# Another order of the steps in a fused attention and token-mixing kernel: loads, stores, filling products and the engines of small copies

## The chip, the cores and the metric

The kernel runs on one core of a Trainium2 chip. The core has five engines that run side by side, each with its own queue of instructions: TensorE (matrix products, PE in the profile, its weight loads PEld), VectorE (DVE), ScalarE (ACT), GpSimd (POOL) and SyncE (SP), which here only issues transfers. An engine works its queue in order: an instruction that waits holds up everything behind it on that engine. Sixteen DMA engines move data between HBM and the on-chip memory; transfers are issued from the queues of SyncE, ScalarE and GpSimd. TensorE's results land in eight banks of PSUM and have to be copied out by VectorE or ScalarE. The metric is the time of one execution in microseconds (us), the median of several runs.

## The reference

Eight batches, eight heads, 576 tokens, 64 channels a head; 32 packed queries p a head. Cut to what matters:

```
def sm_attn(qq, kk, vv):
    s = scale * np.matmul(qq, kk.transpose(0, 1, 3, 2))
    a = np.exp(s - np.max(s, axis=-1, keepdims=True))
    a = a / (np.sum(a, axis=-1, keepdims=True) + 1e-09)
    return np.matmul(a, vv)
p_packed = sm_attn(p, k, v)            # 32 packed rows a head
out = sm_attn(q, p_packed, p_packed)   # 576 rows a head
x = out.transpose(0, 2, 1, 3).reshape(B, S, H * D)
wq, wk = x @ w_q, x @ w_k              # 512 -> 64
W_tok = scale * einsum('bsd,btd->bst', wq, wk)
mixed = einsum('bst,btd->bsd', W_tok, x)
result = np.maximum(mixed, 0.0) @ w_out
```

All inputs and the result are float32: q, k and v are 9.4 MB each, the result is 9.4 MB.

## The kernel before, in words

The kernel never forms W_tok; per batch it multiplies small matrices in another association. Its whole program is one written list, `ORDER`: each word is a step, `NAME.batch.part@engine=banks`, issued in that order, so the list sets the order on every engine's queue, while semaphores keep the data dependences between engines. No scheduler changes it. Engines are A (ScalarE), V (VectorE), P (GpSimd); a load without a mark is GpSimd's, a store without one SyncE's. A step on TensorE names the PSUM banks that it writes.

The steps of one batch b, in the order of its data:

- LD.k, LD.v, LD.q (line 154): loads, float32 in HBM, bf16 on chip, all issued from GpSimd's queue. There are four buffers of each. In batch 0 (h, g, r, q) and batch 7 (r, q) a load is cut in halves. LD.O loads the output weights.
- KT (line 255, VectorE): transposes K in blocks. S1 (263, TensorE): scores of the packed queries. X1 (287, ScalarE): exponentials, in two parts into a single buffer. TE (295, VectorE): transposes them. PV (306): product with V and row sums. RC and PP (318, 321, VectorE): division, and the mask of heads. PT (326): transpose.
- QK (331, TensorE): packed rows times both weight matrices; QKE (341) copies the result out of PSUM, QD (344, GpSimd) doubles a part of it.
- QV (351, VectorE): transposes Q. S2 (362, TensorE): scores of Q, in parts of two token groups (.0, .1), one (.2) or four (.3). X2 (375, ScalarE): exponentials. RS and RR (390, 396, VectorE): row sums and reciprocals. In batch 5 HA (385, GpSimd) first adds halves of the rows. AM (401, GpSimd, in one case VectorE): normalises. AT (409, TensorE): transposes the result. AE (421): copies it out.
- WKQ (433): the products with w_k and w_q; WE (456) copies them out. GM (461) and GE (470): the small matrix of the mixer and its copy. Y (473) and YE (481): the next one. MX (488) and MR (494): mixed rows, MR those of the last, remaining rows of a token group; RL, RLF (515, 519) and RLR (522): relu while copying out.
- OT (527): product with the output weights, 128 rows a step, two steps sharing two banks; part 4 is the remainder rows of two batches at once. OE, OEF (545, 548): copies out. ST, STF (555, 590): stores. In batch 7 the last 128 rows are cut in two column pieces, OH, OEH and STH (574, 581, 585), by the table `OHC` in line 11.

`WARM.n=bank` (line 611) is filling: products of a zero tile with itself, n units of 128 columns, whose result nobody reads. `WARM.n.128` issues them 128 columns at a time, otherwise 512.

`HOLD.v7` (line 567) issues a tiny transfer on SyncE's queue that reads the last V buffer, so every store behind it in that queue waits until V of batch 7 has landed. Copies named with line 128 or 132 in the profile are those of the helper `copy` (ScalarE and VectorE), transposes with line 237 those of `blocks`.

Of the kernel before, what the change touches and what calls it, by code (L numbers as in the profile page):

```python
# [650 lines left out]
```

## Time and profile before

| what | us |
|---|---|
| median of 3 runs (104.35 to 104.62) | 104.36 |
| the profiled execution | 104.42 |
| its span, first to last instruction | 102.6 |
| TensorE busy | 93.2 |
| of it filling products (line 617) | 20.0 |
| VectorE busy | 73.5 |
| ScalarE busy | 65.0 |
| GpSimd busy | 53.1 |

The page divides the span in 40 slices of 2.6 us and shows, for each, the busy share of every engine in tenths, the granted clock of TensorE, the busy share of the DMA engines and the GB/s. In lists of groups, a row has the line and engine, the names of output and inputs, how many instructions, their busy time and mean duration, and the idle time in front of them with what ended it. In a timeline a row begins with start and duration; the bracket at its end is the idle time of the engine before it and who ended that. In a table of windows the columns are the length, the busy time of PE, PEld, DVE, ACT and POOL with their instructions, the granted clock, the DMA share and GB/s.

### The profile page before, as it was taken

The page shows a single profiled execution, that of the slowest core. Times are in us where ns is not written, and L with a number is a line of the kernel's source. Part 1 is how long each engine was busy: PE and PEld are TensorE (multiplying, and loading weights), DVE is VectorE, ACT ScalarE, POOL GpSimd, SP SyncE. Part 2 cuts the span into 40 slices and gives each one's busy share as a digit, 9 for nine tenths or more (in the row PEclk, how much of TensorE's full clock was granted, in tenths as well). Part 3 has the DMA queues.
Part 4 walks back from the last instruction along what each step waited for, and adds up shares of the span by engine and source line. Part 5 has one row for each costly group of instructions (what it writes and reads, how often), then busy time and mean ns, then how long its engine had stood idle before and what let it go on. Part 6 is the DMA issues. An engine that isn't in the chain of part 4 may idle for free.

```text
span 102.6 us, 3594 instructions
## 1 busy us (share of the span) xinstructions
PE 93.2 (91%) x1536; PEld 55.1 (54%) x1536; DVE 73.5 (72%) x140; ACT 65.0 (63%) x111; POOL 53.1 (52%) x83
## 2 busy tenths in 40 slices
PE   5998999998699999999998899989999999999930
...
DMA  1999999999999999999999999999999999997893
GB/s 18 234 230 207 211 215 209 207 210 213 203 212 207 214 209 209 213 210 207 212 210 208 211 212 204 216 211 205 250 250 387 412 413 409 417 388 294 346 370 127
DMA packets 13567, 25.13 MB, mean 245 GB/s; under 512 B 1072, under 2 KB 6448, under 8 KB 13552
## 3 DMA queue, kind: packets, MB, share of 16 engines
...
## 4 chain that ended last, share of the span: by engine, by line
PE 64%; DVE 9%; ACT 8%; DMA 7%; POOL 4%; issue 3%; DVEq 0%; POOLq 0%; ACTq 0%
PE ps L540 26%; PE ps L617 9%; DMA k_sb<-in_k_dram 7%; PE ps L373 5%; PE ps L315 4%; ACT e1T L293 4%; POOL a L405 4%; PE ps L282 3%; PE ps L419 3%; PE ps L446 3%; PE ps L467 3%; DVE rs L394 2%; PE ps L441 2%; PE ps L336 2%; DVE kT L237 2%
## 5 line engine op out<-in xcount | busy, mean ns | idle before, releaser
L540 PE MATMUL ps<-wout,relu 128*128 128x512 bf16 x124 | 30.6, 380 | 0.0
L405 POOL TENSOR_TENSOR a<-e,rr 128x256 bf16<-128x256 f32 (+2 forms) x18 | 19.5, 1099 | 16.4 <-DVE rr L399 6.4
L617 PE MATMUL ps<-o 128*128 128x128 f32 (+3 forms) x76 | 20.0, 410 | 1.2 <-DVE o L135 1.2
L540 PEld LDWEIGHTS <-relu 128*128 128x128 bf16 x124 | 10.7, 98 | 11.7 <-issue 1.1
L128 ACT ACTIVATE o<-ps 128x1024 f32<-128x1024 f32 (+2 forms) x13 | 11.3, 870 | 5.4 <-PE ps L540 5.2
L617 PEld LDWEIGHTS ps<-o 128*128 128x128 f32 x76 | 11.8, 217 | 5.2 <-issue 3.6
L503 ACT ACTIVATE relu<-ps 128x1024 bf16<-128x1024 f32 (+1 forms) x14 | 12.9, 966 | 1.1 <-PE ps L492 1.1
L293 ACT ACTIVATE e1T<-ps 128x576 bf16<-128x576 f32 x16 | 9.8, 655 | 5.2 <-PE ps L282 4.6
L378 ACT ACTIVATE e<-ps 128x256 f32<-128x256 f32 (+2 forms) x19 | 11.2, 622 | 2.5 <-PE ps L373 2.4
L394 DVE TENSOR_REDUCE rs<-e 128x16 f32<-128x512 f32 (+2 forms) x13 | 10.9, 841 | 2.3 <-ACT e L378 2.2
L173 POOL DMA_DIRECT2D v_sb<-in_v_dram x16 | 10.0, 629 | 4.2 <-DMA v_sb<-in_v_dram 1.6
L237 DVE STREAM_TRANSPOSE kT<-k_sb 128x1152 uint32<-128x1152 uint32 (+1 forms) x9 | 11.0, 1226 | 1.4 <-DMA k_sb<-in_k_dram 1.3
L237 DVE STREAM_TRANSPOSE qT<-q_sb 128x1152 uint32<-128x1152 uint32 (+1 forms) x10 | 11.0, 1104 | 0.0
L132 DVE COPY o<-ps 128x1024 f32<-128x1024 f32 (+2 forms) x7 | 6.7, 977 | 5.2 <-PE ps L540 2.7
L237 DVE STREAM_TRANSPOSE e<-e1T 128x288 uint32<-128x288 uint32 x16 | 7.4, 468 | 3.1 <-ACT e1T L293 2.6
L128 ACT ACTIVATE aT<-ps 128x128 bf16<-128x128 f32 (+2 forms) x11 | 5.0, 464 | 5.7 <-PE ps L419 3.3
L128 ACT ACTIVATE wkq<-ps 128x448 bf16<-128x448 f32 (+1 forms) x10 | 7.2, 729 | 1.8 <-PE ps L446 1.7
L315 PE MATMUL ps<-v_sb,e 64*64 64x192 bf16 x288 | 7.5, 245 | 0.8 <-DVE e L237 0.5
L315 PEld LDWEIGHTS <-e 64*64 64x64 bf16 x288 | 5.9, 107 | 2.6 <-DVE e L237 2.0
L373 PEld LDWEIGHTS <-qT 64*128 64x128 bf16 x320 | 5.4, 94 | 2.6 <-DVE qT L237 1.5
L446 PE MATMUL ps<-aT,pqk 128*128 128x256 bf16 (+1 forms) x48 | 6.8, 246 | 0.0
L373 PE MATMUL ps<-ppT,qT 64*128 64x64 bf16 x320 | 6.6, 190 | 0.1
...
## 6 DMA issues: line engine op xcount, KB each, us to landing
v_sb<-in_v_dram POOLq DMA_DIRECT2D x16, 288.0 KB, 14.5
...
k_sb<-in_k_dram POOLq DMA_DIRECT2D x7, 576.0 KB, 14.0
q_sb<-in_q_dram POOLq DMA_DIRECT2D x6, 576.0 KB, 13.5
...
q_sb<-in_q_dram POOLq DMA_DIRECT2D x4, 288.0 KB, 10.5
...
```

What stands on the lines that cost most here:

```text
L128: nc.scalar.activation(o, i, COPY)
L173: nc.gpsimd.dma_start(v_bufs[b % NL][halves(i), 0:7:2], src)
L237: nc.vector.transpose(o, i)
L293: nc.scalar.activation(e1T[:, x], T["s1", b][x].rearrange("a c m -> a m c"), EXP, scale=scale)
L315: nc.tensor.matmul(T["pv", b][halves(cc), i], lhsT, rhs, start=n == 0, stop=n == R - 1, skip_group_check=True)
L373: nc.tensor.matmul(ps[:, y, t - t0, i], lhsT, rhs, start=e == 0, stop=e == 1)
L378: nc.scalar.activation(e2[:, t0:t1].rearrange("a t (i y n) -> a y (t i) n", i=2, y=2), T["s2", b, c].rearrange("a y t i n -> a y (t i) n") ...
L394: nc.vector.tensor_reduce(rs[:, t0 * H:t1 * H], src, axis=AX, op=ADD)
L405: e.tensor_tensor(a2[:, t0:t1].rearrange("a t i (u l) -> a (t i u) l", l=L), e2v(b, c), T["rr", b][:, t0 * H:t1 * H].to_broadcast((P, (t1 ...
L503: nc.scalar.activation(o, i, RELU)
L540: nc.tensor.matmul(ps, lhsT, wout[:, j, :], start=j == 0, stop=j == NJ - 1)
L617: nc.tensor.matmul(bank(int(bk), [w]), warm[:, 0:P], rhs, start=True, stop=True)
```

## The change

The code that makes the steps is the same. `ORDER` is another list, and the two column pieces in `OHC` change their numbers; the list runs piece 1 first in the new order, so the 384 columns still come ahead of the 128.

- The same loads, with k4 ahead of v3, and in batch 7 the second half of Q (r7, q7) ahead of v7. In the first ten microseconds k2 and v1 are issued ahead of two setup steps and of the copies of the weights.
- 25 filling products of 128 columns for 22 ahead of the first scores, and behind them 55 units of 128 columns in fifteen places for 43 in ten.
- S1.1 stands ahead of AT.0.1, S1.2 ahead of GM.0; MR.0, MX.0, MR.1 and others move by a few steps. QK.4 and QK.5 move behind later steps. OT.1 and OT.5 are distributed in another way.
- Copies change engines. From VectorE to ScalarE: AE.2.2, AE.7.1, GE.1, GE.4, GE.6, OE.0.1, OE.3.1, OE.5.0, OE.6.0, OEF.7.1, QKE.1, QKE.3, QKE.5, RLR.6, WE.1.0, YE.0. From ScalarE to VectorE: AE.1.0, AE.4.2, AE.7.0, GE.7, OE.1.1, QKE.6, QKE.7, RL.1.1, RLR.0, RLR.1, WE.7.1, YE.1, YE.7.
- GpSimd's stores were ST.1.4 (batch 1's remainder rows), ST.1.1, ST.0.1, ST.3.0, ST.5.1; they are ST.1.4, ST.3.0, ST.1.0, ST.2.1, ST.5.4. The first of them stands behind the last load, v7, where it stood ahead of Q of batch 7. SyncE's stores are the rest, in another order, with batch 5's ahead of batch 6's.

```diff
--- before.py
+++ after.py
@@ -8,52 +8,53 @@
 NL, NB, NO, NE = 4, 3, 6, 2
 DIAG = ()
 TURN = tuple(range(8))
-OHC = (0, 384), (384, 512)
+OHC = (384, 512), (0, 384)
 
 ORDER = """
 LD.N0@A LD.N1@S SET.warm@V SET.v0@V SET.aT0@V SET.aT1@V SET.aT2@V SET.idf@V LD.W0@A LD.W1@S SET.tab@A LD.h0
-LD.g0 LD.v0 LD.r0 LD.q0 LD.k1 NC.0@V PX.0@V NC.1@A PX.1@V SET.aff@P SET.idb@V SET.v3@P KT.0.0@V SET.mask@P
-WC.1@P WC.0@P LD.k2 SET.v1@P LD.v1 SET.v2@P KT.0.1@V WARM.4=0 WARM.22.128=0 S1.0=0,1,2,3 X1.0.1@A TE.0.1@V
-X1.0.0@A TE.0.0@V WARM.8=4 PV.0.0=4,5 PV.0.1 RC.0@V PP.0.0@V PP.0.1@V LD.q1 PT.0@V WARM.6=6 QK.0=6 QKE.0@A
-QV.0.0@V QV.0.1@V QD.0@P WARM.4=7 S2.0.2=2,3 X2.0.2@A RS.0.2@V RR.0.2@V S2.0.0=0,1 LD.v2 S2.0.1=4,5 X2.0.0@A
-RS.0.0@V RR.0.0@V X2.0.1@A RS.0.1@V RR.0.1@V AM.0.2@P WARM.6=7 AT.0.2=7 AE.0.2@A AM.0.0@P WARM.5=6 AT.0.0=6
-KT.1.2@V AM.0.1@P WARM.3=2 AT.0.1=7 AE.0.1@A AE.0.0@V WKQ.0.0=2,3 WKQ.0.2 WE.0.0@A LD.q2 WKQ.0.1 KT.2.2@V
-S1.1=0,1,4,5 WE.0.1@A GM.0=6 X1.1.0@A TE.1.0@V GE.0@A WARM.2=7 Y.0=2,3 YE.0@V S1.2=0,1,6,7 MR.0=2,3 X1.1.1@A
-TE.1.1@V MX.0.0=4,5 X1.2.0@A LD.O PV.1.0=0,1 TE.2.0@V PV.1.1 X1.2.1@A TE.2.1@V RC.1@V LD.k3 PP.1.0@V PP.1.1@V
-PT.1@V MX.0.1=6,7 QV.1.2@V RLR.0@A QK.1=2 QKE.1@V RL.0.0@A WARM.3=3 S2.1.2=4,5 S2.1.0=0,1 RL.0.1@A X2.1.2@A
-RS.1.2@V RR.1.2@V S2.1.1=2,3 X2.1.0@A RS.1.0@V RR.1.0@V WARM.1=6 PV.2.0=6,7 PV.2.1 X2.1.1@A RS.1.1@V RC.2@V
-LD.v3 QD.1@P AM.1.2@P AT.1.2=4 RR.1.1@V AM.1.0@P WARM.5=5 AT.1.0=5 AM.1.1@P LD.k4 PP.2.0@V AE.1.2@A PP.2.1@V
-PT.2@V QK.2=4 AE.1.0@A QKE.2@A QD.2@P QV.2.2@V LD.q3 LD.v4 AT.1.1=0 AE.1.1@A WKQ.1.0=2,3 WKQ.1.2 WKQ.1.1
-WE.1.0@V S2.2.2=6,7 WE.1.1@A X2.2.2@A S2.2.3=4,5 X2.2.3@A GM.1=1 OT.0.0=2,3 GE.1@V Y.1=6,7 OT.0.1 YE.1@A
-RS.2.4@V OE.0.0@A MR.1=0,1 MX.1.1=4,5 RLR.1@A RR.2.4@V OT.0.2=6,7 LD.q4 OT.0.3 KT.3.2@V AM.2.3@P OE.0.1@V
-RL.1.1@A S1.3=2,3,0,1 X1.3.0@A AM.2.2@P OT.1.4=4 TE.3.0@V LD.k5 AT.2.2=5 X1.3.1@A TE.3.1@V AT.2.3=2 AE.2.3@V
-LD.v5 MX.1.0=6,7 AE.2.2@V PV.3.0=0,1 PV.3.1 OEF.1.4@A WKQ.2.0=2,3 WKQ.2.1 RC.3@V PP.3.1@V RL.1.0@A WKQ.2.2
-WE.2.2@A OT.1.2=4,5 OT.1.3 PP.3.0@V PT.3@V QK.3=6 OE.1.1@A LD.q5 KT.4.2@V S1.4=0,1,2,3 GM.2=7 OT.1.0=4,5
-X1.4.1@A LD.k6 GE.2@A QKE.3@V X1.4.0@A QV.3.2@V TE.4.1@V Y.2=2,3 YE.2@A S2.3.2=6,7 X2.3.2@A S2.3.3=0,1
-X2.3.3@A MX.2.0=2,3 TE.4.0@V RL.2.0@A MR.2=6,7 RLR.2@V OT.1.1 MX.2.1=6,7 RL.2.1@A OE.1.0@A PV.4.0=0,1 QD.3@P
-PV.4.1 RS.3.4@V RR.3.4@V LD.v6 AM.3.3@P AM.3.2@P RC.4@V OT.2.0=2,3 OT.2.1 LD.q6 OE.2.0@A PP.4.0@V PP.4.1@V
-PT.4@V QK.4=6 AT.3.3=7 QV.4.2@V AT.3.2=0 AE.3.2@A LD.k7 S2.4.2=4,5 AE.3.3@V X2.4.2@A S2.4.3=2,3 X2.4.3@A
-KT.5.2@V WKQ.3.0=0,1 WKQ.3.1 WKQ.3.2 RS.4.4@V RR.4.4@V QKE.4@A WE.3.2@A S1.5=4,5,2,3 X1.5.1@A LD.v7 TE.5.1@V
-OT.2.2=6,7 AM.4.3@P QD.4@P AM.4.2@P GM.3=0 X1.5.0@A TE.5.0@V GE.3@A OT.2.3 Y.3=2,3 YE.3@V PV.5.0=4,5 PV.5.1
-HOLD.v7 MR.3=0,1 RC.5@V PP.5.1@V OE.2.1@A MX.3.0=2,3 PP.5.0@V PT.5@V MX.3.1=6,7 RLR.3@A RL.3.0@A OT.3.4=0
-RL.3.1@A AT.4.2=1 AE.4.2@A OEF.3.4@A QV.5.2@V AT.4.3=5 AE.4.3@V ST.1.4@P QK.5=4 QKE.5@V QD.5@P S2.5.2=2,3
-X2.5.2@A KT.6.2@V S2.5.3=6,7 X2.5.3@A HA.5@P WKQ.4.0=0,1 WKQ.4.2 LD.q7 WKQ.4.1 WE.4.2@A OT.3.0=2,3
-S1.6=4,5,6,7 X1.6.0@A GM.4=0 GE.4@V TE.6.0@V LD.r7 OT.3.1 X1.6.1@A TE.6.1@V Y.4=0,1 OE.3.0@A RS.5.4@V RR.5.4@V
-PV.6.0=4,5 YE.4@A PV.6.1 MX.4.0=6,7 RC.6@V RL.4.0@A PP.6.0@V AM.5.3@P PP.6.1@V PT.6@V MX.4.1=2,3 AM.5.2@P
-OT.3.2=0,1 OT.3.3 RL.4.1@A QK.6=4 QKE.6@A QV.6.2@V ST.2.1 S2.6.2=6,7 X2.6.2@A S2.6.3=2,3 ST.3.4 MR.4=4,5
-X2.6.3@A OE.3.1@V RLR.4@V KT.7.2@V AT.5.2=6 AE.5.2@A AT.5.3=7 OT.4.0=0,1 OT.4.1 AE.5.3@A WKQ.5.0=4,5 WKQ.5.2
-OE.4.0@A ST.1.1@P WKQ.5.1 RS.6.4@V WE.5.2@A RR.6.4@V ST.4.0 ST.0.1@P S1.7=2,3,6,7 X1.7.1@A AM.6.3@V ST.3.0@P
-OT.4.2=0,1 GM.5=4 TE.7.1@V OT.4.3 AT.6.3=5 X1.7.0@A TE.7.0@V GE.5@A OE.4.1@A AM.6.2@P AT.6.2=4 ST.2.0 Y.5=6,7
-YE.5@A ST.0.0 ST.3.1 PV.7.0=2,3 QV.7.1@V AE.6.3@V QV.7.0@V AE.6.2@A QD.6@P PV.7.1 RC.7@V PP.7.0@V PP.7.1@V
-PT.7@V MR.5=0,1 RLR.5@A MX.5.1=6,7 RL.5.1@A MX.5.0=4,5 RL.5.0@V WKQ.6.0=0,1 WKQ.6.1 WKQ.6.2 WE.6.2@A OT.5.4=2
-OEF.5.4@A S2.7.1=6,7 ST.5.4 ST.1.0 GM.6=3 GE.6@V X2.7.1@A RS.7.1@V RR.7.1@V S2.7.2=0,1 X2.7.2@A S2.7.0=4,5
-QK.7=2 X2.7.0@A RS.7.0@V RR.7.0@V Y.6=6,7 YE.6@A OT.5.2=0,1 MX.6.1=4,5 QKE.7@A MX.6.0=6,7 AM.7.1@P RS.7.2@V
-RR.7.2@V MR.6=2,3 OT.5.3 RLR.6@V RL.6.0@V RL.6.1@A OE.5.1@A ST.4.1 AM.7.0@P OT.5.0=2,3 AM.7.2@P AT.7.0=4
-AE.7.0@A AT.7.1=5 AE.7.1@V AT.7.2=6 AE.7.2@V OT.6.2=0,1 OEF.6.2@A QD.7@P WKQ.7.0=4,5 WKQ.7.2 WKQ.7.1 WE.7.0@A
-WE.7.1@A STF.6.2 OT.6.0=6,7 OT.6.1 GM.7=0 OE.6.0@V OT.5.1 OE.5.0@V ST.5.1@P GE.7@A Y.7=4,5 OT.6.3 OEF.6.3@V
-ST.6.0 STF.6.3 YE.7@A ST.5.0 MR.7=6,7 RLR.7@A MX.7.0=4,5 RLF.7.0.1@A RLF.7.0.0@V MX.7.1=2,3 RLF.7.1.0@A
-OT.7.4=0 OEF.7.4@A ST.7.4 RLF.7.1.1@V OT.7.1=6 OEF.7.1@V OT.7.0=7 STF.7.1 OT.7.2=1 OEF.7.0@A OH.7.0=0 STF.7.0
-OEF.7.2@A STF.7.2 OEH.7.0@V STH.7.0 OH.7.1=5 OEH.7.1@A STH.7.1@A
+LD.g0 LD.v0 LD.r0 LD.q0 LD.k1 NC.0@V PX.0@V NC.1@A PX.1@V SET.aff@P SET.idb@V KT.0.0@V KT.0.1@V LD.k2 SET.v3@P
+SET.v1@P WARM.4=0 WARM.25.128=0 S1.0=0,1,2,3 X1.0.1@A LD.v1 X1.0.0@A TE.0.1@V WC.0@P TE.0.0@V WARM.8=4
+PV.0.0=4,5 PV.0.1 RC.0@V SET.mask@P PP.0.1@V PP.0.0@V PT.0@V WC.1@P LD.q1 WARM.6=6 QK.0=6 QV.0.0@V SET.v2@P
+QV.0.1@V LD.v2 QKE.0@A WARM.4=7 S2.0.2=2,3 X2.0.2@A S2.0.0=0,1 RS.0.2@V LD.q2 RR.0.2@V AM.0.2@P QD.0@P
+X2.0.0@A RS.0.0@V RR.0.0@V AM.0.0@P S2.0.1=4,5 X2.0.1@A RS.0.1@V RR.0.1@V WARM.6=7 AT.0.2=7 WARM.5=6 AT.0.0=6
+AE.0.2@A KT.1.2@V WARM.2=2 S1.1=2,3,0,1 X1.1.0@A AM.0.1@P AT.0.1=7 AE.0.1@A LD.O AE.0.0@V WKQ.0.0=4,5 WKQ.0.2
+WARM.2=6 WKQ.0.1 KT.2.2@V S1.2=2,3,6,7 WE.0.0@A TE.1.0@V X1.1.1@A TE.1.1@V WE.0.1@A GM.0=4 X1.2.0@A TE.2.0@V
+GE.0@A WARM.2=0 PV.1.0=0,1 PV.1.1 LD.k3 RC.1@V Y.0=2,3 PP.1.0@V PP.1.1@V X1.2.1@A TE.2.1@V YE.0@A WARM.2=5
+MX.0.1=4,5 MR.0=6,7 PT.1@V RL.0.1@A RLR.0@V MX.0.0=2,3 LD.k4 WARM.1=0 QK.1=0 RL.0.0@A QKE.1@A QV.1.2@V
+WARM.6=1 S2.1.2=6,7 X2.1.2@A RS.1.2@V RR.1.2@V AM.1.2@P S2.1.0=4,5 X2.1.0@A RS.1.0@V S2.1.1=2,3 WARM.4=1
+PV.2.0=0,1 PV.2.1 AT.1.2=6 RR.1.0@V X2.1.1@A RS.1.1@V RR.1.1@V RC.2@V PP.2.0@V PP.2.1@V PT.2@V AM.1.0@P
+WARM.4=7 AT.1.0=7 WARM.1=4 QK.2=4 AE.1.2@A AM.1.1@P QKE.2@A AT.1.1=6 AE.1.1@A AE.1.0@V QD.1@P WKQ.1.0=2,3
+QV.2.2@V WKQ.1.2 WE.1.0@A WKQ.1.1 WE.1.1@A LD.v3 S2.2.2=0,1 X2.2.2@A S2.2.3=4,5 X2.2.3@A RS.2.4@V RR.2.4@V
+GM.1=7 GE.1@A OT.0.0=2,3 OT.0.1 OE.0.0@A OT.0.2=0,1 OT.0.3 OE.0.1@A Y.1=4,5 KT.3.2@V WARM.2=6 S1.3=6,7,2,3
+X1.3.0@A LD.q3 LD.v4 LD.q4 YE.1@V MR.1=4,5 MX.1.0=0,1 AM.2.3@P AM.2.2@P X1.3.1@A LD.k5 AT.2.3=6 RLR.1@V
+OT.1.4=7 AT.2.2=4 RL.1.0@A AE.2.2@A KT.4.2@V S1.4=2,3,0,1 MX.1.1=4,5 QD.2@P OEF.1.4@A AE.2.3@V WKQ.2.0=6,7
+WKQ.2.1 TE.3.0@V X1.4.0@A TE.3.1@V WKQ.2.2 WE.2.2@A PV.3.0=2,3 RL.1.1@V LD.v5 PV.3.1 OT.1.2=4,5 RC.3@V
+PP.3.0@V PP.3.1@V X1.4.1@A GM.2=6 OT.1.3 GE.2@A PT.3@V QK.3=7 QKE.3@A TE.4.1@V Y.2=0,1 YE.2@A QV.3.2@V
+S2.3.2=2,3 X2.3.2@A S2.3.3=6,7 QD.3@P MX.2.0=0,1 X2.3.3@A RL.2.0@A OE.1.1@V MX.2.1=2,3 OT.1.0=4,5 OT.1.1
+MR.2=6,7 RL.2.1@A TE.4.0@V OE.1.0@A RS.3.4@V RR.3.4@V LD.q5 LD.k6 PV.4.0=0,1 PV.4.1 RLR.2@V AM.3.3@P RC.4@V
+PP.4.0@V PP.4.1@V PT.4@V OT.2.0=2,3 OT.2.1 OE.2.0@A AM.3.2@P LD.v6 AT.3.3=6 AT.3.2=7 QV.4.2@V S2.4.2=4,5
+X2.4.2@A S2.4.3=0,1 AE.3.3@V WKQ.3.0=2,3 AE.3.2@A KT.5.2@V X2.4.3@A RS.4.4@V LD.q6 RR.4.4@V WKQ.3.1 WKQ.3.2
+WE.3.2@A AM.4.3@P S1.5=4,5,6,7 OT.2.2=0,1 X1.5.1@A AM.4.2@P X1.5.0@A TE.5.1@V TE.5.0@V LD.k7 GM.3=2 OT.2.3
+GE.3@A Y.3=6,7 YE.3@V PV.5.0=4,5 OE.2.1@A PV.5.1 MR.3=2,3 RLR.3@A MX.3.1=6,7 RL.3.1@A MX.3.0=0,1 RL.3.0@A
+QK.4=2 AT.4.3=3 RC.5@V PP.5.1@V PP.5.0@V QKE.4@A OT.3.4=5 AT.4.2=4 QV.5.2@V QD.4@P OEF.3.4@A PT.5@V S2.5.2=6,7
+LD.r7 X2.5.2@A S2.5.3=0,1 X2.5.3@A HA.5@P LD.q7 AE.4.3@V WKQ.4.0=2,3 WKQ.4.1 AE.4.2@V WKQ.4.2 OT.3.0=4,5 LD.v7
+KT.6.2@V S1.6=6,7,0,1 WE.4.2@A GM.4=2 X1.6.1@A TE.6.1@V X1.6.0@A TE.6.0@V OT.3.1 HOLD.v7 GE.4@A QK.5=3 QKE.5@A
+Y.4=0,1 ST.1.4@P YE.4@A OE.3.0@A ST.3.0@P RS.5.4@V RR.5.4@V PV.6.0=6,7 PV.6.1 MX.4.1=2,3 RC.6@V PP.6.0@V
+PP.6.1@V RL.4.1@A PT.6@V MX.4.0=0,1 RL.4.0@A OT.3.2=4,5 QV.6.2@V OT.3.3 QK.6=6 QKE.6@V OE.3.1@A AM.5.3@P
+MR.4=2,3 RLR.4@V S2.6.3=0,1 X2.6.3@A S2.6.2=6,7 AT.5.3=4 X2.6.2@A AM.5.2@P QD.6@P AT.5.2=5 KT.7.2@V AE.5.3@A
+OT.4.0=2,3 OT.4.1 QD.5@P WKQ.5.0=0,1 ST.1.0@P AE.5.2@A WKQ.5.2 OE.4.0@A RS.6.4@V WKQ.5.1 WE.5.2@A S1.7=6,7,4,5
+OT.4.2=2,3 GM.5=0 X1.7.0@A OT.4.3 QV.7.0@V RR.6.4@V AM.6.3@V ST.2.1@P AT.6.3=1 TE.7.0@V X1.7.1@A GE.5@A
+TE.7.1@V AM.6.2@P AT.6.2=0 Y.5=6,7 OE.4.1@A PV.7.0=4,5 PV.7.1 QV.7.1@V YE.5@A MR.5=2,3 AE.6.2@A RLR.5@A ST.4.1
+ST.3.4 AE.6.3@V MX.5.1=6,7 RL.5.1@A RC.7@V PP.7.0@V WKQ.6.0=0,1 PP.7.1@V WKQ.6.1 WKQ.6.2 MX.5.0=2,3 ST.0.1
+PT.7@V S2.7.1=4,5 WE.6.2@A X2.7.1@A OT.5.4=6 RL.5.0@V RS.7.1@V RR.7.1@V ST.3.1 GM.6=7 GE.6@A S2.7.2=0,1
+X2.7.2@A S2.7.0=4,5 ST.1.1 OEF.5.4@A Y.6=2,3 QK.7=7 QKE.7@V OT.5.0=0,1 YE.6@A MR.6=6,7 X2.7.0@A ST.0.0 RLR.6@A
+MX.6.1=2,3 RS.7.2@V RR.7.2@V MX.6.0=4,5 RS.7.0@V RR.7.0@V OT.5.1 OE.5.0@A RL.6.0@V QD.7@P AM.7.2@P AM.7.0@P
+OT.5.2=6,7 AT.7.2=4 AE.7.2@V AT.7.0=5 ST.2.0 AE.7.0@V OT.5.3 AM.7.1@P AT.7.1=0 WKQ.7.0=4,5 RL.6.1@A OT.6.0=2,3
+AE.7.1@A WKQ.7.1 ST.5.0 WKQ.7.2 WE.7.1@V OE.5.1@A WE.7.0@A OT.6.1 ST.5.1 GM.7=1 GE.7@V OE.6.0@A OT.6.2=6,7
+ST.5.4@P Y.7=4,5 OT.6.3 YE.7@V MR.7=0,1 ST.4.0 OEF.6.2@A STF.6.2 OEF.6.3@V MX.7.0=2,3 MX.7.1=4,5 RLR.7@A
+RLF.7.0.0@V OT.7.4=6 ST.6.0 RLF.7.0.1@A RLF.7.1.1@V RLF.7.1.0@A OT.7.2=7 OEF.7.4@A OEF.7.2@A STF.6.3 OT.7.1=0
+ST.7.4 STF.7.2 OT.7.0=1 OEF.7.1@A OH.7.1=0 STF.7.1 OEF.7.0@A STF.7.0 OEH.7.1@A STH.7.1@A OH.7.0=3 OEH.7.0@V
+STH.7.0
 """
 
 
```

## The prediction

> **What bounds the kernel now.** I read the page first: the busy row, the 40 slices, and the group of line 617, the filling products.
>
> ```profile
> PE 93.2 (91%) x1536; PEld 55.1 (54%) x1536; DVE 73.5 (72%) x140; ACT 65.0 (63%) x111; POOL 53.1 (52%) x83
> ...
> PE   5998999998699999999998899989999999999930
> ...
> DMA  1999999999999999999999999999999999997893
> ...
> L617 PE MATMUL ps<-o 128*128 128x128 f32 (+3 forms) x76 | 20.0, 410 | 1.2 <-DVE o L135 1.2
> ```
>
> Two things are full from start to end: TensorE and the DMA engines. TensorE's 93.2 us hold 20.0 us of filling. Next I asked for windows.
>
> ```profile
> 9.30:24.00 14.70, 14.14 (x243) 7.51 (x242) 9.71 (x20) 6.14 (x13) 11.48 (x18) 1.00 1.15 210
> 24.00:41.00 17.00, 15.06 (x310) 8.47 (x282) 13.70 (x27) 11.26 (x21) 9.58 (x13) 1.00 1.16 209
> 41.00:58.00 17.00, 16.01 (x336) 9.43 (x335) 14.20 (x25) 13.55 (x21) 9.53 (x14) 1.00 1.14 210
> 58.00:79.00 21.00, 20.47 (x408) 12.19 (x409) 18.55 (x32) 18.33 (x30) 12.92 (x16) 1.00 1.13 237
> 79.00:98.50 19.50, 19.41 (x238) 10.50 (x226) 13.04 (x26) 13.33 (x26) 3.53 (x5) 1.00 0.96 383
> ```
>
> The first column after the length is TensorE's busy time, the third from the end its granted clock, 1.00 throughout, then the DMA share. From the first scores (9.3) to PV of batch 7 (79) it is idle 0.56+1.94+0.99+0.53 = 4.0 us, and fills take 11.9 us (20.0 less the 8.1 at the start, quoted below), the last in front of AT.1.0 at 32. So up to 41 waits set the pace, from 58 on TensorE does. Behind PV.7 it is full (19.41 of 19.50): what delays PV.7 delays the end.
>
> The loads give the other bound. I asked for the DMA issues of narrow windows; the last column is the time from issue to landing. The first row is k3 (window 21.8 to 22.5), the second k4 (32.8 to 33.0), the third the halves of batch 7's Q (66.6 to 68.0). The fourth is HOLD on SyncE's queue, which waits for v7.
>
> ```profile
> k_sb<-in_k_dram POOLq DMA_DIRECT2D x1, 576.0 KB, 16.3
> ...
> k_sb<-in_k_dram POOLq DMA_DIRECT2D x1, 576.0 KB, 10.9
> ...
> q_sb<-in_q_dram POOLq DMA_DIRECT2D x2, 288.0 KB, 11.0
> ...
> 75.34 0.62 SPq L572 DMA_DIRECT2D touch<-v_sb  x1
> ```
>
> So k3 lands at 38.2, k4 at 43.8, v7 at 75.3 and the last Q at about 67+11 = 78. The engines never run dry on the way (DMA share over 1 in each window), so in any order the same loads end at about 78; only who comes last changes.
>
> **The change, part by part.**
>
> *Three more 128-wide products at the start* (25 for 22).
>
> ```profile
> 1.19 8.14 PE L617 MATMUL ps<-o 128*128 128x512 f32 x46 [1.19 <-DVE o L135]
> 9.05 0.78 DVE L237 STREAM_TRANSPOSE kT<-k_sb 128x576 uint32<-128x576 uint32 x1 [0.96 <-DMA k_sb<-in_k_dram]
> 9.88 0.47 PE L282 MATMUL ps<-kT,pT 32*32 32x288 bf16 x30 [0.33 <-DVE kT L237]
> ```
>
> The fills end at 1.19+8.14 = 9.33. A product is two records, which start 0.11 apart at the end of the run, so three more end 0.67 later, at 10.0 (the last overlaps S1.0 a little). S1.0's second part waited until 9.88 for the other half of K anyway: +0.05 to +0.1.
>
> *Twelve more filling units behind it* (55 of 128 columns for 43; 0.22 each by the two records above, 11.9/43 = 0.28 by their busy time): 2.6 to 3.3 us of product. They are in front of steps that may wait anyway, so their cost lies between 0 and 3.3; it needs the order walked with durations of this trace.
>
> *The front, 10 to 41 us.* Rows of before, ScalarE's copy WE.0 and exponential X1.1.0 first:
>
> ```profile
> 22.10 0.54 ACT L128 ACTIVATE wkq<-ps 128x448 bf16<-128x448 f32 x1 [0.17 <-PE ps L446]
> 22.64 0.65 ACT L293 ACTIVATE e1T<-ps 128x576 bf16<-128x576 f32 x1
> ...
> 26.84 0.31 DVE L237 STREAM_TRANSPOSE ppT<-pp 128x128 uint32<-128x128 uint32 x1
> 27.08 1.34 DVE L237 STREAM_TRANSPOSE qT<-q_sb 128x1152 uint32<-128x1152 uint32 x1
> ...
> 28.47 0.78 PE L373 MATMUL ps<-ppT,qT 64*128 64x64 bf16 x40
> ...
> 32.97 0.23 PEld L419 LDWEIGHTS <-a 128*128 128x128 bf16 x4 [0.34 <-POOL a L405]
> ...
> 36.45 1.49 DVE L394 TENSOR_REDUCE rs<-e 128x40 f32<-128x1280 f32 x1 [0.43 <-ACT e L378]
> ...
> 37.63 0.23 PE L498 MATMUL ps<-wkq,y 64*128 64x64 bf16 x4
> ...
> 38.01 1.90 PE L540 MATMUL ps<-wout,relu 128*128 128x512 bf16 x8
> 38.48 1.38 DVE L237 STREAM_TRANSPOSE kT<-k_sb 128x1152 uint32<-128x1152 uint32 x1
> ...
> 39.92 0.48 PE L282 MATMUL ps<-kT,pT 32*32 32x288 bf16 x32
> ```
>
> S1.1 moves ahead of AT.0.1 and starts as soon as KT.1 is done, at 20.4. On ScalarE the order is now X1.1.0 (20.95 to 21.6), AE.0.1 (to 22.2), WE.0.0 (to 22.7), X1.1.1 (to 23.35), WE.0.1 (to 23.9); WE.0.1 was done at 22.64. GM.0 stands behind S1.2, which TensorE has through at 23.0, and waits 0.9 for it. PV.1 follows at 24.6, hardly earlier than before. On VectorE TE.2.1 (a transpose of 0.5) now stands behind PP.1, and RLR.0 (0.4, ScalarE's before) ahead of QV.1: RC.1 at 25.6, PP.1 to 26.4, TE.2.1 to 26.9, PT.1 to 27.2, RLR.0 to 27.6, so QV.1 starts at 27.55 instead of 27.08. S2.1 comes at 29.1, where the six fill units ahead of it end, for 28.47. The chain softmax, row sums, GpSimd's product, transposes, copies moves with it: GpSimd's last of three products ends at 33.55, AT.1.1 starts at 33.75 for 32.97. The copies WE.1.0 and WE.1.1 are both ScalarE's now and end at 35.95, ahead of X2.2; so RS.2.4 starts at 37.35 for 36.45, KT.3 (1.38) at 39.35, S1.3 at 40.8: +0.9. MR.1 and MX.1.1 (37.63 to 38.01, 0.38 together) stood before S1.3 and stand behind it now. TensorE is thus 1.25 us behind. Bounds: 0, if every fill lies in a wait and S1.3 comes at 39.6 (k3 at 38.2 and the transpose of 1.38), with the 0.38 still to do; 3.3 if the fills all lie on the path.
>
> *The middle, 41 to 70.* k4 loads ahead of v3, lands at 41 and lets S1.4 run early, at 43.6; v3 lands where k4 did, at 43.8, and PV.3, fitted behind S1.4 and WKQ.2, comes at 45.2. The waits that before had here are these, GpSimd's product and VectorE's transposes being late:
>
> ```profile
> 53.60 0.41 PE L336 MATMUL ps<-wqk,ppT 64*64 64x128 bf16 x8
> 54.46 0.62 PE L419 MATMUL ps<-idb,a 128*128 128x128 bf16 x8 [0.45 <-POOL a L405]
> ...
> 55.80 1.37 DVE L237 STREAM_TRANSPOSE kT<-k_sb 128x1152 uint32<-128x1152 uint32 x1
> ...
> 57.22 0.49 PE L282 MATMUL ps<-kT,pT 32*32 32x288 bf16 x32 [0.32 <-DVE kT L237]
> ...
> 68.14 0.94 PE L315 MATMUL ps<-v_sb,e 64*64 64x192 bf16 x36 [0.47 <-DVE e L237]
> ```
>
> VectorE is close to full here (14.20 of 17.00), and it paces both orders: QV.4 is done at 55.7, AE.3.3 follows, KT.5 starts at 56.3 for 55.8, S1.5 at 57.7 for 57.22. With QK.4 (0.41, the row at 53.60) put behind it the lag is 0.9. On ScalarE WE.4.2 comes behind both RL.3, QKE.4 and OEF.3.4, so GM.4 waits 0.5 for it: PV.6 at 69.25 for 68.14, lag 1.1. Net of the middle: -0.15; bounds -1.2 (the three waits recovered) to +0.6.
>
> *70 to PV.7.* OE.3.1 goes from VectorE to ScalarE, between RL.4.0 and X2.6.
>
> ```profile
> 69.44 1.94 ACT L503 ACTIVATE relu<-ps 128x1024 bf16<-128x1024 f32 x2 [0.62 <-PE ps L492]
> ...
> 71.56 1.23 DVE L132 COPY o<-ps 128x1024 f32<-128x1024 f32 x1
> ...
> 74.98 1.02 ACT L128 ACTIVATE o<-ps 128x1024 f32<-128x1024 f32 x1 [0.33 <-PE ps L540]
> ```
>
> The copy takes VectorE 1.23, ScalarE about 1.02 (74.98's row), and ScalarE loses QKE.6 (0.38): +0.64, against idle of 0.62+0.33 between its steps, of which the new step uses a part. WE.5.2, X1.7, GE.5, YE.5 and so PV.7 and MR.5 come later by 0 to 0.64; I take the middle, +0.3. PV.7, near 78.8 before, then stands at 80.2. V of batch 7, now the last load, lands at 78.1, before that: no cost, unless it came over 2 us later.
>
> *The tail.* The same steps remain behind PV.7, so TensorE's 19.4 us stay. QV.7.0 and QV.7.1 now run before PV.7 ends, which shortens PT.7's wait by 0.5, but S2.7 stood behind OT.5.4 anyway. OE.6.0, OE.5.0 and OEF.7.1 change from VectorE to ScalarE; a tile of the last group takes TensorE about 1.90/2 = 0.95 (the row at 38.01, two tiles), ScalarE 1.02/2 to copy, so ScalarE keeps up alone. Of the last tile the 384 columns still come first; they now leave by ScalarE's queue and the 128 by SyncE's. Nothing, bounds -0.3 and +0.3.
>
> *Stores and the drain.*
>
> ```profile
> 92.00:94.00 2.00, 1.98 (x18) 0.69 (x16) 2.00 (x3) 0.79 (x3) 0.00 (x0) 1.00 0.66 260
> 94.00:96.00 2.00, 1.97 (x10) 0.90 (x11) 1.36 (x3) 1.55 (x3) 0.00 (x0) 1.00 0.80 309
> ...
> out_dram<-o SPq DMA_DIRECT2D x1, 192.0 KB, 2.5
> out_dram<-o ACTq DMA_DIRECT2D x1, 64.0 KB, 2.8
> ```
>
> From 92 to 96 the stores run short of data (0.66 and 0.80 of the engines), about 1.1 us lost. ST.5.0, among the last stores in SyncE's queue before, now stands ahead of batch 6's, so less is queued at the end: the 64 KB store that took 2.8 behind others should take 2.5 or a little more. -0.2 (0 to -0.4). Of the 9.4 MB to store none may start before the loads are nearly through; HOLD.v7 opens SyncE's queue at 78 instead of 75.3, but GpSimd's four stores fill the engines meanwhile, so the engines stay full across that moment and the order of who fills them costs nothing.
>
> [...]
>
> *Sum.* +1.25 (front, the start in it) -0.15 (middle) +0.3 (ScalarE) +0 (tail) -0.2 (drain) = +1.2. Durations are of one execution, 102.6 us of span and 104.42 in all, 0.06 above the median of 104.36: 104.4+1.2 = 105.6.
>
> **The rivals.**
>
> 1. *Faster: the lag is given back before PV.7.* TensorE's steps from S1.0 to PV.7 are those of before and twelve fills, 2.6 to 3.3 us; of the 4.0 of idle of before about 1.0 is left. If the new order idles less than that, PV.7 comes as early as v7 allows, 78.1 for 78.8. For it: the many short fills look like measured waits. Against: waits of 0.9 (GM.0) and 0.5 (GM.4) that I find in the walk. Time: 104.4-0.6-0.2 = 103.6, the 0.6 from PV.7. It decides from an idle of 1.0 down; the walk has 2.3.
> 2. *No difference:* the loads pace both orders, the front's lag is absorbed by the waits at 54 to 57 and 68 (1.2 together): 104.4.
> 3. *Slower still: GpSimd issues loads too late.* LD.q5 stands behind QD.3, LD.q7 and LD.v7 behind QD.4 and HA.5, which waits for X2.5. The first load of all (window 1.2 to 1.4, nothing ahead of it) shows what a load needs from issue to landing:
>
> ```profile
> k_sb<-in_k_dram POOLq DMA_DIRECT2D x1, 288.0 KB, 5.7
> ```
>
> LD.v7 goes out at some 69, to land at 78, so it has 3 us in hand. If ScalarE is over 3 us late there, each further us is one of the end; or all twelve fills lie on the path. Time: 106.8.
>
> **How the numbers follow.** This kernel's runs tell 0.3% from no change, 0.3 us. Forecast (105.6, itself 104.8 to 106.3) 0.52, rival 1 0.22, rival 2 0.10, rival 3 0.16. Slower 0.68, same 0.10, faster 0.22. The range reaches from just above rival 1 to rival 3: 103.8 to 106.8.
>
> **What would show it.** Right: PV.7 at about 80, S1.3 at 40.8, QV.1 at 27.5, GM.0 and GM.4 waiting for ScalarE's copy (line 128), batch 7's V landing at 78, TensorE full behind PV.7. Wrong: S1.3 by 39.7, less than 1.0 us of idle from 10 to 79; or DMA slices below 9 before slice 29.

## The result and the profile after

The changed kernel takes 105.35 us in the median (105.23 to 105.54) beside 104.35 (104.31 to 104.62) for the kernel before in the same runs: a ratio of 1.0083, interval 1.0065 to 1.0100. It is slower, by about the forecast amount. Ratios here and below leave out executions that took over 1.5% more than the fastest of their kernel. The profiled execution of after took 105.54, its span 103.8; so the spans differ by 1.11 us. Line numbers of after are those of before plus one.

The page of after, its busy row, the slices of TensorE and of the DMA engines, and the group of the filling products:

```profile
PE 96.5 (93%) x1552; PEld 58.3 (56%) x1552; DVE 70.1 (68%) x137; ACT 67.0 (65%) x114; POOL 53.1 (51%) x83
...
PE   5999999998999999898899899999999999999940
...
DMA  2999999999999999999999999999999699999974
...
L618 PE MATMUL ps<-o 128*128 128x128 f32 (+2 forms) x92 | 25.3, 420 | 1.2 <-DVE o L136 1.2
```

TensorE has 5.3 us more of filling, and the DMA engines have a hole, the 6 in slice 31, counted from 0 (80.4 to 83.0 us). The same windows as before, and one of the hole:

```profile
9.30:24.00 14.70, 14.64 (x246) 8.42 (x245) 9.51 (x20) 5.38 (x12) 10.31 (x20) 1.00 1.15 210
24.00:41.00 17.00, 16.49 (x264) 9.73 (x262) 11.97 (x25) 10.84 (x21) 7.97 (x11) 1.00 1.16 209
41.00:58.00 17.00, 15.82 (x334) 9.43 (x333) 14.71 (x25) 12.48 (x21) 9.38 (x14) 1.00 1.15 210
58.00:79.00 21.00, 20.58 (x425) 12.16 (x424) 17.89 (x31) 19.56 (x31) 14.25 (x19) 1.00 1.13 237
79.00:98.50 19.50, 19.45 (x246) 10.82 (x245) 12.02 (x25) 15.29 (x28) 3.89 (x6) 1.00 0.94 366
...
80.00:82.00 2.00, 2.00 (x62) 1.50 (x60) 1.80 (x6) 1.84 (x5) 0.00 (x0) 1.00 0.37 143
```

TensorE's idle time from 9.3 to 79 is 0.06+0.51+1.18+0.42 = 2.2 us, where it was 4.0. The steps by which the prediction wanted to be judged, from timelines of after (start, duration, step):

```profile
1.19 9.60 PE L618 MATMUL ps<-o 128*128 128x512 f32 x52 [1.19 <-DVE o L136]
10.72 0.48 PE L283 MATMUL ps<-kT,pT 32*32 32x288 bf16 x32
...
24.44 0.34 PE L468 MATMUL ps<-wkq,a 128*128 128x64 bf16 x6 [0.27 <-ACT wkq L129]
...
27.86 1.36 DVE L238 STREAM_TRANSPOSE qT<-q_sb 128x1152 uint32<-128x1152 uint32 x1
...
41.11 0.48 PE L283 MATMUL ps<-kT,pT 32*32 32x288 bf16 x32
...
49.48 1.06 PE L374 MATMUL ps<-ppT,qT 64*128 64x64 bf16 x40 [0.47 <-DVE qT L238]
...
67.46 0.47 PE L468 MATMUL ps<-wkq,a 128*128 128x64 bf16 x10
...
78.55 0.60 SPq L573 DMA_DIRECT2D touch<-v_sb  x1
80.71 0.63 SPq L562 DMA_DIRECT2D out_dram<-o  x1
...
80.14 0.91 PE L316 MATMUL ps<-v_sb,e 64*64 64x192 bf16 x36
```

In order: the fills end at 10.79 (9.33 before), S1.0, GM.0 with a wait of 0.27 for ScalarE's copy WE.0.1, QV.1, S1.3 at 41.11 (39.92 before), S2.3, GM.4 without a wait, HOLD behind V of batch 7, SyncE's first store, and PV.7 at 80.14 (78.79 before). The last issues, from 97 us on, with their time to landing:

```profile
out_dram<-o SPq DMA_DIRECT2D x3, 256.0 KB, 2.5
...
out_dram<-o ACTq DMA_DIRECT2D x1, 192.0 KB, 2.6
out_dram<-o SPq DMA_DIRECT2D x1, 64.0 KB, 2.0
```

### The profile page after: what moved, and what is told of

Same layout as the page of the kernel before. It is cut to its first block, busy times and chain, and to the rows that moved or that the text cites. A ratio compares the mean times of both kernels' runs of the same rounds, so it can differ in the third digit from the quotient of the medians.

```text
span 103.8 us, 3616 instructions
## 1 busy us (share of the span) xinstructions
PE 96.5 (93%) x1552; PEld 58.3 (56%) x1552; DVE 70.1 (68%) x137; ACT 67.0 (65%) x114; POOL 53.1 (51%) x83
## 4 chain that ended last, share of the span: by engine, by line
PE 77%; DVE 7%; ACT 7%; issue 2%; POOL 2%; ACTq 0%; DVEq 0%; POOLq 0%
PE ps L541 24%; PE ps L618 22%; PE ps L316 6%; PE ps L374 5%; PE ps L420 4%; PE ps L283 3%; PE ps L447 3%; ACT e1T L294 3%; PE ps L493 2%; PE ps L442 2%; PE ps L337 2%; POOL a L406 2%; PE ps L468 2%; DVE rs L395 1%; DVE kT L238 1%
## 5 line engine op out<-in xcount | busy, mean ns | idle before, releaser
L618 PE MATMUL ps<-o 128*128 128x128 f32 (+2 forms) x92 | 25.3, 420 | 1.2 <-DVE o L136 1.2
L129 ACT ACTIVATE o<-ps 128x1024 f32<-128x1024 f32 (+2 forms) x17 | 15.2, 894 | 6.3 <-PE ps L541 5.9
L618 PEld LDWEIGHTS ps<-o 128*128 128x128 f32 x92 | 14.8, 225 | 5.7 <-issue 3.9
L504 ACT ACTIVATE relu<-ps 128x1024 bf16<-128x1024 f32 (+1 forms) x13 | 11.9, 958 | 0.5 <-PE ps L499 0.5
L131 POOL COPY pqk<-pqk 128x128 bf16<-128x128 bf16 x8 | 2.3, 289 | 12.5 <-DVE pqk L133 6.3
L442 PE MATMUL ps<-pqk,aT 128*128 128x64 bf16 x80 | 6.2, 194 | 0.3 <-ACT aT L129 0.2
```

The costliest lines, as they stand in the source:

```text
L129: nc.scalar.activation(o, i, COPY)
L504: nc.scalar.activation(o, i, RELU)
L618: nc.tensor.matmul(bank(int(bk), [w]), warm[:, 0:P], rhs, start=True, stop=True)
```

## The experiments

Twelve kernels. The starts below are read from the timelines; "last" is the start of the last column piece on TensorE (OH).

| kernel | PV.0 | S1.3 | PV.7 | last | span | ratio to before (interval) |
|---|---|---|---|---|---|---|
| before | 12.21 | 39.92 | 78.79 | 98.14 | 102.65 | 1 |
| after | 13.07 | 41.11 | 80.14 | 99.47 | 103.76 | 1.0083 (1.0065 to 1.0100) |
| fill22 | 12.17 | 40.21 | 79.07 | 98.39 | 103.12 | 1.0053 (1.0028 to 1.0077) |
| front_before | 12.65 | 40.89 | 81.18 | 100.51 | 105.05 | 1.0229 (1.0212 to 1.0245) |
| front_after | 12.69 | 40.93 | 80.05 | 99.41 | 103.66 | 1.0069 (1.0052 to 1.0086) |
| no_late_fills | 12.40 | 41.29 | 80.56 | 99.88 | 104.74 | 1.0114 (1.0068 to 1.0159) |
| front_before_k4 | 12.22 | 40.14 | 78.92 | 98.24 | 103.09 | 1.0073 (1.0046 to 1.0101) |
| before_25 | 12.27 | 40.70 | 79.58 | 98.94 | 103.17 | 1.0022 (0.9991 to 1.0053) |
| after_18 | 12.16 | 40.20 | 78.95 | 98.28 | 103.15 | 1.0043 (1.0016 to 1.0070) |
| front_dve | 12.10 | 40.12 | 79.34 | 98.67 | 103.44 | 1.0039 (1.0014 to 1.0063) |
| queue_18 | 12.30 | 40.34 | 79.08 | 98.41 | 103.07 | 1.0073 (1.0046 to 1.0099) |
| last_18 | 12.30 | 40.48 | 79.24 | 98.57 | 103.29 | 1.0050 (1.0022 to 1.0078) |
| queue_last_18 | 12.34 | 40.50 | 79.26 | 98.59 | 103.32 | 1.0071 (1.0040 to 1.0102) |
| before_18 | 12.11 | 40.27 | 79.59 | 98.95 | 103.23 | 1.0104 (1.0052 to 1.0155) |

None beats the kernel before.

**fill22: the start alone.**

```diff
-WARM.25.128=0
+WARM.22.128=0
```

> The changed kernel with 22 filling products at the start instead of 25. In its profile the first scores began at 10.72 us, 1.46 later than before, where 0.67 was forecast, because TensorE's full clock was granted at 7.2 us instead of 5.6. Theory A (the loss of 1.0 us is made by the order between 20 and 37 us: ScalarE's copy WE.0.1 late, TE.2.1 and RLR.0 ahead of QV.1): the start is nearly absorbed, 105.25, 0.1 below the changed kernel. Theory B (the start is the loss, the 0.86 us by which batch 0 lies later there): 104.5.

PV.0 came back to 12.17 and PV.7 to 79.07, 1.07 earlier; the ratio came from 1.0083 to 1.0053 only, a third of a microsecond. The reason stands in the fills' own rows. Records per window, before first, then after:

```profile
4.00:5.50 1.50, 1.50 (x9) 1.50 (x9) 0.71 (x2) 0.00 (x0) 1.50 (x3) 1.00 1.07 265
5.50:7.20 1.70, 1.70 (x17) 1.70 (x17) 0.81 (x2) 0.63 (x1) 1.49 (x8) 1.00 1.12 237
```

```profile
4.00:5.50 1.50, 1.50 (x9) 1.50 (x9) 0.64 (x2) 0.00 (x0) 1.50 (x3) 1.00 1.06 243
5.50:7.20 1.70, 1.70 (x10) 1.70 (x10) 1.13 (x4) 0.63 (x1) 1.68 (x5) 1.00 1.11 230
```

In the second window before runs 17 records and after 10. The first entry on the granted clock in the trace, at full speed, stands at 5.57 us in before and at 7.22 in after; ahead of it the products run slower (in both, their records start 0.21 us apart, behind it 0.11), and the table's 1.00 says nothing about them. That moment is not the kernel's: over the fourteen profiles of this study it lies between 4.04 and 7.25, in no relation to the order. With 25 products the fills end at 10.12 when it comes at 5.81, at 10.27 for 6.13 and at 10.79 for 7.22; so 1 us later costs 0.47. At before's 5.57, then, 25 products would end at 10.0, as forecast, and in before_25, where it came at 5.53, they end at 9.99. And the first scores have a floor, the other half of K, as fill22's timeline shows, where the clock came early:

```profile
1.19 7.45 PE L617 MATMUL ps<-o 128*128 128x512 f32 x46 [1.19 <-DVE o L135]
...
9.84 0.44 PE L282 MATMUL ps<-kT,pT 32*32 32x288 bf16 x22 [0.97 <-DVE kT L237]
```

So with 22 products an execution has slack against a late clock, with 25 hardly any. PV.0 stays at 12.1 to 12.3 where the fills end by about 10.0 and goes up with them from there (12.40 for 10.12, 12.69 for 10.27, 13.07 for 10.79). The one exception is front_before: its fills end at 8.60, but the other half of K is late there (S1.0's second part at 10.32 for 9.88), and PV.0 comes at 12.65. An estimate from these numbers: with the moment spread evenly between 4.04 and 7.25, three products cost 0.25 us on average, and 0.86 in the one execution that was profiled.

**front_before and front_after: which part of the order.** Before's list up to S2.2.3, after's behind it, and the reverse:

```diff
 WE.1.1@A X2.2.2@A S2.2.3=4,5
-X2.2.3@A GM.1=1 OT.0.0=2,3 GE.1@V Y.1=6,7 OT.0.1 YE.1@A RS.2.4@V
+X2.2.3@A RS.2.4@V RR.2.4@V GM.1=7 GE.1@A OT.0.0=2,3 OT.0.1 OE.0.0@A
...
```

> The kernel before up to S2.2.3 (36 us), with its 22 and 43 filling units, and all later steps in the changed order, on the changed engines. Theory A and theory B: the loss is ahead of 37 us, so 104.3 to 104.4, no different from before. Theory C (the loss comes from the middle or the tail, ScalarE's additional copies among it): 105.0 to 105.4.

> The mirror image: the changed kernel up to S2.2.3, then the order of before. Theories A and B: 105.3 to 105.5. Theory C: 104.4. If the two halves don't add up to the 1.0 us, the lag of the front is partly absorbed by the middle in one of the orders: then 104.8 to 105.1.

front_before, at 107.04, is the slowest of all and fits none of the theories, from a cause that neither whole order has. TensorE's waits from 40 to 50 us, and the load of k4, issued at 33.63:

```profile
PE ps L282 <- DVE kT L237: 1.4, 1, 1.4
...
33.63 0.77 POOL L176 DMA_DIRECT2D k_sb<-in_k_dram  x1
...
k_sb<-in_k_dram POOLq DMA_DIRECT2D x1, 576.0 KB, 10.1
```

k4 lands at 43.7; after's steps want S1.4 at 43 and put PV.3 behind it, while before loads v3 first. So the comparison of halves was spoilt by its seam. front_after needs from PV.0 to S2.2.2 (35.35) 22.66 us, as after does (35.73 less 13.07); before needs 22.30 (34.51 less 12.21). Its second half, before's, gave nothing back; 105.38 is what theories A and B said, the loss lying ahead of 37 us.

**front_before_k4: the seam mended.**

```diff
-LD.v3 QD.1@P AM.1.2@P ... AM.1.1@P LD.k4
+LD.k4 QD.1@P AM.1.2@P ... AM.1.1@P LD.v3
```

> The run front_before again with one thing else: k4 is loaded ahead of v3, as in the changed kernel, where the kernel before loads v3 first. In front_before S1.4 came at 45.2 and PV.3, which stands behind S1.4 in the changed order, at 46.9, although S1.3 was as early as in the changed kernel. Theory: the changed order of S1.4 and PV.3 needs the changed order of these two loads, and the 1.7 us over the changed kernel are k4's landing at 43.8. Then S1.4 comes by 44 and the time is 104.6 to 105.1. Rival: another seam (banks, engines of the copies) made it slow; then 106.5 to 107 again.

The two loads, exchanged, take 2.26 us off PV.7, part of it the later start of the kernel without (0.43): TensorE is as early as before nearly to the end (78.92; last piece 98.24), and yet the span is 0.44 longer. With before's front, the steps from S1.3 on cost TensorE nothing; what is left of the loss in this execution comes behind TensorE. The profiled execution took 104.96, within the expected range, but the median is 105.38, above it; what the slower executions lose isn't in the trace.

**no_late_fills: are the filling units on the path?** All units behind AE.0.2 are left out, 26 of 128 columns; nothing reads them.

```diff
-WARM.2=2 ... WARM.2=6 ... WARM.2=0 ... WARM.2=5 ... WARM.1=0 ... WARM.6=1 ... WARM.4=1 ... WARM.4=7 ... WARM.1=4 ... WARM.2=6
```

> The changed kernel without the ten fills from WARM.2=2 on (26 units of 128 columns, 5.6 to 7 us of product), those between the first transposes of batch 0 and S1.3. Theory A (order and chains of copies set the pace; the fills lie in waits or nearly so): 105.0 to 105.3, with TensorE's idle time up by 5 us and S1.3 at 40.5 to 41. Theory D (the fills themselves stand on the path): 104.3 or less, S1.3 by 40. Should the granted clock fall without them, slower than the changed kernel: 106 or more.

Slower, as the expectation's third case said: 106.32 in the median, because the clock fell. The profiled execution took 106.52 with a mean granted clock of 0.967; four of the other five have 0.966 to 0.968 (105.92 to 106.86), and one has 0.983 and took 104.86. The clock was halved from 29.70 to 36.53; TensorE's busy time and granted clock in a window half as long ahead of that stretch, and in its two halves:

```profile
26.29:29.70 3.41, 1.86 (x57) 1.00 1.18 210
29.70:33.11 3.41, 2.55 (x42) 0.50 1.18 208
33.11:36.53 3.42, 3.40 (x58) 0.50 1.14 210
```

The clock is 0.50 in both halves, behind a window in which TensorE was busy for 1.86 of 3.41 us. In the same window of before it was busy for longer, in after all the time, and neither lost its clock; before first, then after:

```profile
26.29:29.70 3.41, 2.49 (x56) 1.00 1.18 210
```

```profile
26.29:29.70 3.41, 3.41 (x30) 1.00 1.18 210
```

The busy share of one such window alone doesn't decide, though. In front_before, waiting for k4, TensorE was busy for less than half of a window of the same length and kept its clock, and before_18 kept it behind 1.85 us (8.03 to 11.44):

```profile
41.58:45.00 3.42, 1.65 (x15) 1.00 1.12 211
45.00:48.41 3.41, 3.16 (x88) 1.00 1.19 209
```

What does decide stays open. Up to the halving the kernel without these units reaches PV.2 17.1 us behind PV.0, after 18.3 and before 17.4; so the units do stand on TensorE's path there. From PV.2 on the halved clock hides what they cost, and how much of the +0.33 of after's front is theirs stays open; what they give is the clock: 0.995 to 1.0 in after's four executions. The one execution that lost only half as much of it, 104.86, is below all of after's (105.23 to 105.54), which is a hint, from a single run, that with the clock kept the kernel would be faster without these units.

**front_dve: the copies and transposes that change engine in the front** (on top of fill22).

```diff
-RC.1@V Y.0=2,3 PP.1.0@V PP.1.1@V X1.2.1@A TE.2.1@V
+X1.2.1@A TE.2.1@V RC.1@V Y.0=2,3 PP.1.0@V PP.1.1@V
...
-RL.0.1@A RLR.0@V
+RLR.0@A RL.0.1@A
...
-QKE.1@A QV.1.2@V
+QV.1.2@V QKE.1@V
...
-WE.1.0@A
+WE.1.0@V
```

> The changed kernel with 22 products at the start (fill22) and, in the front, the engines and the order of VectorE as before: TE.2.1 ahead of RC.1, RLR.0 on ScalarE, QKE.1 and WE.1.0 on VectorE. Theory A (QV.1 0.5 late through TE.2.1 and RLR.0, and the copies WE.1 in line on ScalarE, carry the lag of the order): 104.6 to 104.8, 0.4 below fill22, S1.3 0.4 to 0.7 earlier against PV.0. Rival (fills or TensorE itself decide there): 105.1 to 105.3 like fill22.

From PV.0 to S1.3 it needs 28.02, fill22 28.04, after 28.04, before 27.71. The four edits change nothing: the chain over VectorE that the prediction made the front's cost does not carry it. The rival of the expectation (TensorE itself decides there) is what the windows from PV.0 to S1.3 show, before first, then after:

```profile
12.21:39.92 27.71, 25.53 (x454) 1.00 1.15 209
```

```profile
13.07:41.11 28.04, 27.47 (x458) 1.00 1.15 210
```

After's TensorE has 1.94 us more to do in the front and waits 1.61 less (0.57 for 2.18): that is the +0.33. Its filling products are busy for 13.66 us there, before's for 9.89. So in the front TensorE is all but full with its own work, the added units among it. How much shorter the front would be with fewer of them is shown by no run: in no_late_fills, the only one without them, the clock fell. Two of TensorE's waits in front_dve:

```profile
PE ps L373 <- issue: 0.3, 1, 0.3
...
PE ps L467 <- ACT wkq L128: 0.3, 1, 0.3
```

GM.0's wait for WE.0.1 (line 467) is there as in after, 0.3. It does not make the lag: after_18 has no wait at GM.0, S1.2 in front of it waits 0.21 for its transpose of K instead, and the front takes 28.04 all the same. The other is in the middle of S2.3: there after's profile, too, takes 1.06 us for 40 products that take 0.78 elsewhere, 0.28 more for nothing that the trace shows; after_18, queue_18 and last_18, with the same steps there, take 0.77 or 0.78, fill22 0.88.

**before_25, before_18 and after_18: the number of products in either order.**

```diff
-WARM.22.128=0
+WARM.25.128=0
```

```diff
-WARM.22.128=0
+WARM.18.128=0
```

```diff
-WARM.25.128=0
+WARM.18.128=0
```

> The kernel before with 25 filling products at the start for 22, and nothing else. It measures the start alone. My step: 0.05 to 0.1 at most, 104.5 to 104.7 where the kernel before has 104.6. Rival: the clock is granted at 4.0 to 7.2 us, another time in each execution, and with 25 products a late grant puts the first scores at 10.7; the delay goes through to the end, so 104.9 in the median, 105.4 in the slowest run.

> Before's order with 18 filling products in place of 22. Theory start (the end of the filling products, which moves with the moment at which the clock is granted, sets when the first scores may begin, and 3 products are worth 0.2 to 0.5 us): PV.0 at 12.1 at the latest, 104.1 to 104.4, ratio 0.995 to 0.999. Rival (the first loads set it, products are free): 104.5, ratio 1.000; 25 products gave 1.0022 with an interval that holds 1.

> The changed kernel with 18 products at the start. With these the fills end before K is transposed (9.8 us) at whatever moment the clock is granted, so what is left over the kernel before is the order alone. If the order costs what its profile shows beside the start (PV.0 to PV.7 67.07 us for 66.58), 0.4 to 0.5: 105.0 to 105.1. If the start was all of it: 104.6. The runs should lie closer together than those of fill22 (104.7 to 105.8).

after_18 halves the loss, 1.0043 for 1.0083, and its median, 105.07, is the one expected. before_25 has 104.93 in the median, as its rival said, but with a ratio of 1.0022 whose interval holds 1. before_18 missed its expectation: PV.0 came at 12.11 as expected, and the kernel is slower, not faster. Its ratio of 1.0104 mixes two kinds of executions. Three of the six kept the clock (1.0) and took 104.96 to 105.25, 0.4 to 0.7 above before's median of 104.55. The other three have a mean granted clock of 0.976 to 0.979 and took 106.29 to 106.79. This goes with the 18 products: over all kernels with 18, 14 of 54 executions have a mean clock below 0.98, and of 135 with 22 or 25 none has (no_late_fills left out). No profile was taken of one of the 14, so where they lose the clock isn't shown.

For the executions with the clock kept there are two rows of VectorE's timeline, first before_25, then before_18:

```profile
15.95 0.78 DVE L237 STREAM_TRANSPOSE qT<-q_sb 128x576 uint32<-128x576 uint32 x1 [0.76 <-DMA q_sb<-in_q_dram]
```

```profile
27.39 1.38 DVE L237 STREAM_TRANSPOSE qT<-q_sb 128x1152 uint32<-128x1152 uint32 x1 [0.34 <-DMA q_sb<-in_q_dram]
```

Each waits for a load that before's profile has in time; TensorE lost 0.70 (S2.0) and 0.46 (S2.1) by it, and before_18 another 0.47 inside PV.6 and behind it. So in each of these executions a load landed late for its step, by 0.76 and by 0.34, and these two steps had no slack for that. Whether fewer products shift the loads or the executions only differ is open; at any rate the start that is 0.1 earlier brought no gain.

**queue_18, last_18 and queue_last_18: the end of the stores** (all on top of after_18). The first takes away the hole at 80 us, the second exchanges the queues of the last two stores, the third does both.

```diff
-HOLD.v7
+HOLD.q7
...
-ST.4.1 ST.3.4 ... ST.0.1 ... ST.3.1 ... ST.1.1
+ST.3.4 ... ST.0.1 ... ST.3.1 ... ST.1.1 ST.4.1
```

```diff
-STH.7.1@A STH.7.0
+STH.7.1 STH.7.0@A
```

> After's order with 18 filling products (ratio to before 1.0043 in its own run), and in SyncE's store queue two moves: ST.4.1 stands behind ST.1.1, so that stores whose data are ready are no longer queued behind one that waits for ScalarE's OE.4.1; and the hold waits for q7 (lands 75.7) in place of v7 (78.5). Theory H (the hole of the DMA engines between 79.5 and 82 us is what ends after's order late, once TensorE is as early as before): from 79 to 84 us about 2.05 MB move in place of 1.77 MB, span 102.7, time 104.5 to 104.7, ratio 0.999 to 1.001. Theory L (the hole is made up for by 95 us, where the DMA engines run dry in every kernel of this case, and what is late is the last two stores, which the change put on the other queues): the hole goes, the engines run dry earlier at 93 to 95.5 us, and span 103.1, time 105.0 and ratio 1.004 stay.

> After's order with 18 filling products, and only the last two stores exchanged between queues as before has them: the 192 KB by SyncE, the 64 KB by ScalarE. Theory L: the last DMA packet ends 2.35 us behind the last issue as in before, in place of 2.76; span 102.7 to 102.8, time 104.6 to 104.7, ratio 1.000 to 1.001. Theory H: 105.0, ratio 1.004, with the hole at 80 to 82 us as it was.

> Both edits together. If H or L alone holds, as that one's run; if each holds a part, 104.3 to 104.5. If it comes out at 105.0 as well, neither is what ends after's order late and the cause stays open.

Windows of after_18, then of queue_18; the last column is GB/s:

```profile
79.00:84.00 5.00, 4.95 (x130) 3.56 (x128) 3.99 (x10) 4.50 (x10) 0.00 (x0) 1.00 0.92 354
84.00:92.00 8.00, 7.90 (x70) 4.31 (x70) 4.54 (x10) 6.09 (x10) 3.52 (x5) 1.00 1.00 395
```

```profile
79.00:84.00 5.00, 5.00 (x134) 3.67 (x132) 4.08 (x9) 4.49 (x10) 0.00 (x0) 1.00 1.02 408
84.00:92.00 8.00, 8.00 (x71) 4.34 (x72) 4.53 (x10) 6.09 (x10) 3.52 (x5) 1.00 0.92 369
```

The hole is gone, the engines run short of data later instead, and span and ratio get no better (103.1, and 1.0073 for 1.0043): theory H falls. last_18 and queue_last_18 have spans of 103.3, where theory L wanted 102.7 to 102.8: theory L falls with its own edit.

What the end consists of shows when the reports of the last store are taken one by one. The trace has sixteen for each of these stores; I take them as one from each of the 16 DMA engines. In before the fifteenth report of the store that lands last comes at 101.45, 3.31 behind the last piece's start, and the sixteenth 0.23 later; the span ends 0.97 after that. The first term is 3.3 in after (3.30), fill22, front_before_k4, after_18 and queue_18 as well (3.31 to 3.32). The second is what differs: 0.02 in after, 0.02 to 0.03 in front_after, before_25 and before_18, 0.37 in queue_18, 0.44 and 0.45 in fill22 and last_18, 0.55 and 0.57 in front_before_k4 and after_18. By this reading one of the sixteen engines is behind the others, and the program waits for it. The rows of after_18's last stores show it as a longer landing, beside those of after above:

```profile
out_dram<-o SPq DMA_DIRECT2D x3, 256.0 KB, 3.3
out_dram<-o ACTq DMA_DIRECT2D x1, 192.0 KB, 3.2
out_dram<-o SPq DMA_DIRECT2D x1, 64.0 KB, 2.6
```

From the last piece to the end of the span the kernels that end in after's list with an early TensorE (fill22, front_before_k4, front_dve and the four with 18 products) take 4.66 to 4.87, which is 0.15 to 0.36 more than before's 4.51; after itself, late as it is, takes 4.29. But before's own profile is a long one: before_25, before_18 and front_after, with the same list at the end, take 4.23 to 4.28. Why that engine is more behind in this order (nine of its ten kernels have 0.25 to 0.57, the four that end in before's list 0.02 to 0.23) is not settled.

## Why the prediction was right, and where its steps were not

The time came out as forecast, 105.35 for 105.6, and the ends of the sum too: PV.7 at 80.14 for "then stands at 80.2", the tail (from PV.7 to the last piece 19.35 before, 19.33 after), the drain. The frame held: the front runs late, nothing gives it back, and what delays PV.7 delays the end. That the sum came so close is luck: most of the +1.11, the start's 0.86, is what the prediction put at nearly nothing, and it depends on the moment of the clock in that execution; the steps behind it were forecast too large and made up for it. In the profiled execution, with the forecast's steps read from its own times (S1.3 at 40.8 for 39.92, PV.6 at 69.25 for 68.14):

| step | forecast | measured |
|---|---|---|
| start, to PV.0 | +0.05 to 0.1 | +0.86 |
| PV.0 to S1.3 (the front) | +0.8 | +0.33 |
| S1.3 to PV.6 (MR.1 and MX.1.1, 0.38, moved here) | +0.2 | +0.13 |
| PV.6 to PV.7 | +0.3 | +0.03 |
| tail | 0 | -0.02 |
| drain | -0.2 | -0.22 |
| sum | +1.2 | +1.11 |

- **Start.** "S1.0's second part waited until 9.88 for the other half of K anyway" holds, and the 10.0 for the fills' end holds for a clock that comes at 5.57. The step took that moment from one execution as if it belonged to the kernel. In after's it came 1.65 later, worth 0.79; the three products are the other 0.67 of the 1.46 by which the fills end later. In the medians the start is worth less: fill22 is lower by 0.3%, after_18 by 0.4%, with intervals that overlap after's.
- **Front.** "+1.25 us behind" failed in its size and in its reason. The walk gave GM.0 a wait of 0.9; it is 0.27, and in after_18 it is nothing. The chain RC.1, PP.1, TE.2.1, RLR.0, QV.1 was named as what carries the rest, but QV.1 starts 14.79 behind PV.0 in after and 14.87 before, and with TE.2.1 and RLR.0 put back front_dve is unchanged. Measured is +0.33, a steady amount in after, fill22, after_18 and front_dve, and it is TensorE's own products: up to S1.3 it waits 0.57 in all. The prediction had this among its bounds ("if the fills all lie on the path"), not in its sum.
- **Middle.** GM.4's wait of 0.5 for WE.4.2 doesn't exist. Of the +0.13, 0.28 is the time lost inside S2.3, which after_18, queue_18 and last_18 don't have; after_18 has -0.14 here, with the moved 0.38 included.
- **ScalarE, 70 to PV.7.** "I take the middle, +0.3": it was 0.03, the lower bound. ScalarE is busier (19.56 of 21.00 for 18.33), but nothing before PV.7 waits for it.
- **Drain.** The size is right by the executions that were compared: before's slowest engine was 0.23 behind and after's 0.02, while before_25 and before_18 have 0.02 to 0.03 and drains as short as after's. The reason given, ST.5.0 earlier, is not shown. The 64 KB took 2.0 for the 2.5 or a little more that was forecast; it did not end the program, since the 192 KB on ScalarE's queue, 2.6, land later.
- **HOLD.** "The engines stay full across that moment" is wrong: from 80 to 82 us after's DMA engines are busy for only 0.37 of the time, because SyncE's first store waits for OE.4.1 until 80.71 with ready ones behind it. "Costs nothing" is right as far as queue_18 shows; the hole that it took away, after_18's, was a smaller one (0.81 of the time from 80 to 82).
- **Rivals.** TensorE's idle time from 9.3 to 79 is 2.2, the walk had 2.3; rival 1 needed less than 1.0. Rival 2 is excluded by the interval. Rival 3's loads are in time: V of batch 7 has landed by 78.55, where 78.1 was forecast.

For the medians the account is then: about 0.25 by the start (an estimate, above), 0.2 by the order on TensorE (from PV.0 to PV.7 66.79 in after_18, 66.58 in before), up to 0.3 by waits that come and go, and -0.2 to +0.36 by the slowest DMA engine. It is put together from single profiled executions; no run measures this split of the medians.
